# A new written-out order of loads and steps for a packed attention followed by a two-layer MLP

## The chip, the cores and the metric

The kernel runs on one core of a Trainium2 chip. Times are device microseconds (us) of one launch. The engines are TensorE (PE: matrix products; its weight loads are shown as PEld), VectorE (DVE), ScalarE (ACT), GpSimd (POOL) and SyncE (SP). POOL and SP only issue transfers here: POOL the loads, SP the transposing transfers within the chip's memory and the stores. Each engine works through its own queue in order.

## The reference

Eight batches, eight heads, 576 positions, head dimension 64, and 32 "pack" queries p per head:

```python
def sm_attn(qq, kk, vv):
    s = scale * np.matmul(qq, kk.transpose(0, 1, 3, 2))
    a = softmax(s)
    return np.matmul(a, vv)
p_packed = sm_attn(p, k, v)               # 32 rows per head
out = sm_attn(q, p_packed, p_packed)      # 576 rows per head
x = out.transpose(0, 2, 1, 3).reshape(B * S, H * D)   # 4608 x 512
r = np.maximum(x @ w_in, 0.0)             # 4608 x 2048
y = (s * (r * r) + b) @ w_out             # 4608 x 512, f32
```

## The kernel before

The work is a list of words, and each word is a step of one batch. The same function `run` reads the list and issues what the word says; each engine gets its part in the order of the list (the class `Pinned` and the helpers `mm` and `tr`, lines 62, 65 and 73, keep the program order). So the order of every queue is written out by hand, and a word that waits on an engine holds up all later words of that engine, but none of another.

The words, with the batch as first number:

- `Lk`, `Lq`, `Lv`, `Lp`, `Lpall`, `Lwi`, `Lwo`, `Lsb`: loads, issued by POOL. There is one raw buffer each for k, q and v, so a load waits until the batch before has been turned or copied out. Batch 0's loads come in two parts. `Lwi0.1` loads columns 0 to 256 of w_in, `Lwi2.4` 512 to 1024, and so on.
- `Tk`, `Tq`: k or q turned on PE (batches 0 and 1) into PSUM and copied out; `Dk`, `Dq`: turned by a transposing transfer on SP (batches 2 to 7).
- `PD`, `PP`, `PA`, `PPA`: the pack queries doubled and turned; `V`: v copied into the order that the products want (DVE).
- `F` first scores and their exponential (ACT); `P` packed values and their division (DVE); `X` packed values turned; `S` second scores and exponentials; `A` the softmax sums on PE, their logarithm and inverse on ACT, the product with the exponential on DVE. Batch 0 has `e`, `d`, `l`, `i`, `G` for the pieces of S and A.
- `W`: packed values times a quarter of w_in (an eighth in batch 0), copied out by two copies.
- `M` (and `h` in batch 0): 128 of the 2048 hidden columns: four products of 288 columns (h: of 384 where its last number is 0, of 192 where it is 1), a ReLU out of PSUM, a square on DVE.
- `O`: products with w_out for a tile of 128 rows, `xN` of its 16 steps; `Q`: the tile scaled, the bias added (DVE), and stored (SP, two stores a tile). The last tile is done in two halves of 256 columns.
- `BT`: the sums of w_out for the bias. `Z`: idle products on zeros.

`@` names the PSUM banks that a step takes (there are eight), and a trailing `a` or `v` says whether ACT or DVE does the copy or the ReLU. A word named again goes on with the same step: the first `M3.4@2` is its products, `M3.4a` its ReLU, the next `M3.4` its square. At most three ReLU results wait for their square (pool `ysp`), and at most five output tiles for their stores (pool `outp`).

PE's order in the long middle mixes `M` of batch b with `O` of batch b-1, and puts F, P, X, S, W and A of the next batch in between.

Of the kernel before, what the change touches and what calls it, by code (L numbers as in the profile page):

```python
# [14 lines left out]
def kernel(  # L15
# [670 lines left out]
    for word in """  # L686
        Tk0.0@2 Lq0.1 Tk0.0v Tk0.0v PD0 Z2@1 PP0@4 PP0v Tk0.1@6 PP0v Tk0.1a Tk0.1v Z2@5 F0.0@0 F0.0
        F0.1@2 F0.1 V0.0 Z3@4 P0.0@5 P0.0 V0.1 Z4@4 X0.0 X0.0v Z1@4 P0.1 P0.1 Z4@4 X0.1 Tq0.0@6 Tq0.0v
        Tq0.0v Tq0.1@4 S0.0.0@0 Tq0.1v Z2@2 S0.1.0@6 Lwi0.1 X0.1v Tq0.1a S0.1.1 e1.1 W0.0@4 e1.0 Z1@3
        d1.1@2 l1.1 Lp1 d1.0 S0.0.1 l1.0 Lwi6.8 PD1 PP1@6 PP1v e0.0 Z2@7 d0.0@2 PP1v e0.1 d0.1 Z4@7  # L690
        W0.6@0 W0.0v W0.0v W0.6v i1.1 W0.7@4 i1.0 l0.1 i0.1 G0.1 Lwi1.2 l0.0 Z5@6 W0.1@2 i0.0 G0.0 W0.6a
        W0.1a W0.1a G1.1 h0.12.0@0 W0.7a W0.7a h0.0.0@6 h0.0.0a Lwi2.4 G1.0 h0.14.1@2 h0.12.0v h0.12.0
        W0.2@4 W0.2a Lk1 W0.2a h0.14.1v Lv1 h0.2.0@0 h0.14.1 h0.14.0@6 h0.14.0a Lq1 h0.0.0 h0.2.0v
        h0.2.0 h0.4.1@2 h0.4.1v h0.14.0 W0.3@4 W0.3v W0.3a Lwi4.6 h0.4.0@0 h0.4.0a Tk1.0@6 Tk1.0v Tk1.0v
        Tk1.1@2 Tk1.1v Tk1.1a h0.0.1@4 F1.0@0 h0.0.1a F1.0 F1.1@6 h0.4.0 h0.4.1 h0.0.1 h0.6.0@2 h0.2.1@4
        V1 F1.1 h0.12.1@0 P1.1@6 P1.1 X1 h0.6.0a h0.2.1a h0.2.1 h0.12.1v h0.12.1 Lwo0.4 h0.6.1@2 Lsb
        Tq1.1@4 X1a h0.6.1v Tq1.1a Tq1.1a Tq1.0@6 Tq1.0v W1.0@0 h0.6.1 Tq1.0v W1.0v W1.0v S1@2,4 S1 S1
# [97 lines left out]
```

## Time and profile before

| | us |
|---|---|
| median of 3 runs | 250.53 (250.45 to 250.72) |
| the profiled execution | 250.68 |
| its span, first to last instruction | 248.9 |
| PE busy | 237.4 (95%) |
| DVE busy | 165.8 (67%) |
| ACT busy | 121.4 (49%) |
| first product of PE | 1.19 |
| last matrix product ends | 245.24 |

A line of the timeline gives the start, the time from the start of the first to the end of the last of its instructions, the engine, the line of the kernel, what it writes and reads, the shapes and the count; in brackets the idle time before and who ended it. In the list of waits, each line has the engine that waited, whom it waited for, the total, the number of waits and the longest. In the chain that ended last, each piece is the start, its length and the engine or transfer. A line's number can be that of a helper (L62 is every product, L73 every instruction of the other engines). The transfers' landing times that the text gives are those of the same trace.

### The profile page before, as it was taken

The numbers are of one execution on the slowest core, as the hardware profiler recorded it, in microseconds if no ns is written. First come the engines' busy times: TensorE is split into PE (matmuls) and PEld (weight loads), VectorE is DVE, ScalarE is ACT, GpSimd is POOL, SyncE is SP. The second block draws the span as 40 slices with busy tenths as digits, with TensorE's granted clock in tenths as the row PEclk, the third lists the DMA queues.
The fourth block names the chain that finished last, engine by engine and source line by source line (L and its number), as shares of the span: only waits on it lengthen the run. The fifth ranks groups of instructions, "written<-read, shape, count | busy, mean of one in ns | idle before, by whom it ended". The sixth has DMA issues, their size and how long they took to land.

```text
span 248.9 us, 5651 instructions
## 1 busy us (share of the span) xinstructions
PE 237.4 (95%) x2334; PEld 133.9 (54%) x2334; DVE 165.8 (67%) x336; ACT 121.4 (49%) x213; POOL 30.6 (12%) x45
## 2 busy tenths in 40 slices
PE   8889869999799999999999999999999999999994
PEld 3545644655355655476546645574547554675442
DVE  4657989799765856897469854983478724971232
ACT  2347768522464442675158423991278515890000
POOL 8643222001010210102003001020000000000000
PEclk9999999999999999999999999999999999999998
DMA  6999999997995999899999968969239031200135
GB/s 98 170 197 204 204 192 205 203 150 180 144 218 102 200 162 225 156 130 158 170 234 151 228 151 148 186 90 175 78 95 190 2 94 33 61 27 24 45 81 148
DMA packets 60522, 35.53 MB, mean 143 GB/s; under 512 B 32720, under 2 KB 56016, under 8 KB 60496
## 3 DMA queue, kind: packets, MB, share of 16 engines
q0 software_dynamic: 26272, 18.58, 52.8%
q1 hardware_dynamic: 34176, 16.55, 31.5%
q8 instruction: 18, 0.29, 0.5%
q14 instruction: 8, 0.07, 0.1%
q10 hardware_dynamic: 48, 0.03, 0.1%
HBM read 37.23 MB, written 9.44 MB: 187 GB/s over the span
## 4 chain that ended last, share of the span: by engine, by line
PE 76%; DVE 9%; DMA 8%; ACT 2%; POOL 2%; issue 2%; SPq 0%; POOLq 0%; ACTq 0%; DVEq 0%
PE banks L62 76%; DMA w_in_sb<-in_moe_w_in_dram 4%; DMA qT<-qn 3%; DVE gT L73 2%; DVE rlu L73 2%; ACT rlu L73 1%; DVE bias L73 1%; DVE pbd L73 1%; DVE biasrep L73 1%; ACT e L73 1%; POOL qn L73 1%; POOL kn L73 1%; POOL vn L73 1%; DVE ysb L73 1%; DVE kT L73 0%
## 5 line engine op out<-in xcount | busy, mean ns | idle before, releaser
L62 PE MATMUL banks<-w_out_sb,gT 128*128 128x512 bf16 (+1 forms) x592 | 140.9, 374 | 0.0
L62 PEld LDWEIGHTS <-gT 128*128 128x128 bf16 x592 | 55.7, 98 | 54.0 <-issue 4.5
L62 PE MATMUL banks<-aT,pw 128*128 128x288 bf16 (+2 forms) x512 | 74.1, 286 | 1.8 <-DVE rlu L73 0.7
L73 ACT ACTIVATE rlu<-banks 128x576 bf16<-128x576 f32 (+2 forms) x94 | 57.6, 656 | 33.1 <-PE banks L62 19.2
L73 DVE TENSOR_TENSOR gT<-rlu 128x576 bf16<-128x576 bf16 (+2 forms) x128 | 55.4, 454 | 12.7 <-ACT rlu L73 9.5
L62 PEld LDWEIGHTS <-pw 128*128 128x128 bf16 x512 | 49.2, 98 | 24.8 <-issue 2.2
L73 DVE SCALAR_TENSOR_TENSOR ysb<-banks,svec,biasrep 128x512 f32<-128x512 f32 (+1 forms) x37 | 26.8, 732 | 33.5 <-PE banks L62 33.1
L73 ACT ACTIVATE e<-banks 96x768 bf16<-96x768 f32 (+3 forms) x34 | 21.8, 693 | 49.1 <-PE banks L62 49.1
L73 DVE TENSOR_SCALAR rlu<-banks 128x576 bf16<-128x576 f32 (+2 forms) x34 | 25.1, 741 | 6.6 <-PE banks L62 2.9
L73 DVE CAST pw<-banks 128x512 bf16<-128x512 f32 (+1 forms) x37 | 22.3, 634 | 5.5 <-PE banks L62 5.4
L73 ACT CAST pw<-banks 128x512 bf16<-128x512 f32 (+1 forms) x35 | 16.4, 538 | 2.3 <-PE banks L62 2.3
L62 PE MATMUL banks<-zb 128*128 128x512 bf16 x42 | 12.9, 434 | 1.2 <-DVE zb L73 1.2
L73 POOL DMA_DIRECT2D qn<-in_q_dram x9 | 7.0, 776 | 52.5 <-DMA qT<-qn 49.5
L73 DVE TENSOR_TENSOR aT<-e,rcd 128x576 bf16<-128x576 bf16 (+2 forms) x18 | 11.8, 685 | 1.0 <-ACT rcd L73 1.0
L62 PE MATMUL banks<-w_in_sb,ppd 64*32 64x512 bf16 (+1 forms) x288 | 11.2, 357 | 0.9 <-ACT e L73 0.5
L62 PEld LDWEIGHTS <-ppd 64*32 64x32 bf16 x432 | 5.3, 89 | 11.7 <-issue 8.5
L73 POOL DMA_DIRECT2D vn<-in_v_dram x9 | 6.7, 748 | 39.2 <-DVE vr L73 37.4
L73 ACT ACTIVATE ld<-banks 128x576 f32<-128x576 f32 (+2 forms) x18 | 10.2, 596 | 1.6 <-PE banks L62 1.0
L73 POOL DMA_DIRECT2D kn<-in_k_dram x9 | 6.9, 768 | 31.9 <-DMA kT<-kn 28.3
L73 ACT ACTIVATE rcd<-ld 128x576 f32<-128x576 f32 (+2 forms) x18 | 10.7, 630 | 0.3
L73 DVE RECIPROCAL rd<-banks 128x2 f32<-128x2 f32 (+1 forms) x9 | 1.5, 170 | 11.1 <-PE banks L62 10.3
L73 DVE COPY vr<-vn 96x3072 bf16<-96x3072 bf16 (+1 forms) x9 | 7.7, 859 | 1.0 <-DMA vn<-in_v_dram 1.0
(54 smaller groups left out, 98.9 us busy)
## 6 DMA issues: line engine op xcount, KB each, us to landing
out_dram<-ysb SPq DMA_DIRECT2D x23, 192.0 KB, 2.8
kn<-in_k_dram POOLq DMA_DIRECT2D x7, 576.0 KB, 9.7
vn<-in_v_dram POOLq DMA_DIRECT2D x7, 576.0 KB, 11.4
qn<-in_q_dram POOLq DMA_DIRECT2D x7, 576.0 KB, 8.7
out_dram<-ysb SPq DMA_DIRECT2D x24, 128.0 KB, 3.4
w_out_sb<-in_moe_w_out_dram POOLq DMA_DIRECT2D x4, 512.0 KB, 15.4
w_in_sb<-in_moe_w_in_dram POOLq DMA_DIRECT2D x3, 512.0 KB, 12.4
out_dram<-ysb SPq DMA_DIRECT2D x23, 64.0 KB, 2.1
```

Source lines behind the costliest of these rows:

```text
L62: return tc.keep_in_program_order(nc.tensor.matmul(*a, **kw))
L73: return lambda *a, **kw: tc.keep_in_program_order(f(*a, **kw))
```

## The change

Nothing but the list changes, and with it line numbers by one. All steps that compute are there as before; what differs is the order, the banks, which of ACT and DVE does a copy or ReLU (M: 80 on ACT and 32 on DVE, 86 and 26 before; h: 13 and 3, 8 and 8 before), and the idle products (44 in all, the first 12 among them; 42 before). The order of the loads differs too. The opening, cut after the words in which batch 1 is under way:

```diff
-    Tk0.0@2 Lq0.1 Tk0.0v Tk0.0v PD0 Z2@1 PP0@4 PP0v Tk0.1@6 PP0v Tk0.1a Tk0.1v Z2@5 F0.0@0 F0.0
-    F0.1@2 F0.1 V0.0 Z3@4 P0.0@5 P0.0 V0.1 Z4@4 X0.0 X0.0v Z1@4 P0.1 P0.1 Z4@4 X0.1 Tq0.0@6 Tq0.0v
-    Tq0.0v Tq0.1@4 S0.0.0@0 Tq0.1v Z2@2 S0.1.0@6 Lwi0.1 X0.1v Tq0.1a S0.1.1 e1.1 W0.0@4 e1.0 Z1@3
-    d1.1@2 l1.1 Lp1 d1.0 S0.0.1 l1.0 Lwi6.8 PD1 PP1@6 PP1v e0.0 Z2@7 d0.0@2 PP1v e0.1 d0.1 Z4@7
-    W0.6@0 W0.0v W0.0v W0.6v i1.1 W0.7@4 i1.0 l0.1 i0.1 G0.1 Lwi1.2 l0.0 Z5@6 W0.1@2 i0.0 G0.0 W0.6a
-    W0.1a W0.1a G1.1 h0.12.0@0 W0.7a W0.7a h0.0.0@6 h0.0.0a Lwi2.4 G1.0 h0.14.1@2 h0.12.0v h0.12.0
-    W0.2@4 W0.2a Lk1 W0.2a h0.14.1v Lv1 h0.2.0@0 h0.14.1 h0.14.0@6 h0.14.0a Lq1 h0.0.0 h0.2.0v
-    h0.2.0 h0.4.1@2 h0.4.1v h0.14.0 W0.3@4 W0.3v W0.3a Lwi4.6 h0.4.0@0 h0.4.0a Tk1.0@6 Tk1.0v Tk1.0v
-    Tk1.1@2 Tk1.1v Tk1.1a h0.0.1@4 F1.0@0 h0.0.1a F1.0 F1.1@6 h0.4.0 h0.4.1 h0.0.1 h0.6.0@2 h0.2.1@4
-    V1 F1.1 h0.12.1@0 P1.1@6 P1.1 X1 h0.6.0a h0.2.1a h0.2.1 h0.12.1v h0.12.1 Lwo0.4 h0.6.1@2 Lsb
-    Tq1.1@4 X1a h0.6.1v Tq1.1a Tq1.1a Tq1.0@6 Tq1.0v W1.0@0 h0.6.1 Tq1.0v W1.0v W1.0v S1@2,4 S1 S1
-    W0.4@6 W0.4v Lpall Lwo4.8 W0.5@2 W0.5a W0.5v W0.4v Lwo8.12 W1.1@0 A1.0@4 W1.1a h0.10.0@2 W1.1v
-    A1.0 h0.10.1@6 h0.10.1a A1.1@0 A1.1 A1.1 h0.10.0v h0.8.1@4 h0.10.1 A1.0 Lwo12.16 W1.3@6 W1.2@2
-    O0.3x1@0 h0.8.1v O0.3x1 O0.1x1@1 W1.3a W1.3v O0.2x3@4 h0.8.1 O0.3x2 A1.1 O0.1x1 h0.8.0@6 O0.1x2
-    W1.2a W1.2a h0.8.0a h0.10.0 h0.6.0 A1.0 M1.0@2 M1.0a PA O0.2x1 h0.8.0 O0.1x1 M1.3@6 M1.6@2 M1.6v
-    O0.3x2 M1.6 M1.3a Lq2 M1.3 O0.2x1 M1.14@6 M1.14a M1.5@2 O0.3x1 M1.5v M1.5 O0.2x1 PPA0@5,6 M1.9@2
-    PPA0 O0.1x3 M1.9a M1.9 BT@7 M1.4@2 PPA0 O0.3x3 O0.2x1 M1.4a O0.0x2@5 O0.3x3 Lk2 O0.3x1 O0.0x5
 ...
+    Lq0.1 PD0 PP0@1 Tk0.0@2 Tk0.0a Tk0.0a PP0a Z2@0 Tk0.1@4 Tk0.1a PP0v Lp1 Tk0.1v V0.0 Z2@6 F0.0@2
+    F0.0 Z5@7 P0.0@0 P0.0 F0.1@4 F0.1 Lwi0.1 Z1@1 X0.0 X0.0v V0.1 Z4@1 P0.1 P0.1 Tq0.0@2 Tq0.0a
+    Tq0.0v Z2@1 Tq0.1@1 Tq0.1v Tq0.1a X0.1 X0.1v S0.0.0@6 Lwi2.4 Z1@4 S0.0.1 e0.1 S0.1.0@2 S0.1.1
+    Z3@5 d0.1@0 e0.0 d0.0 e1.1 e1.0 W0.0@4 d1.1@6 l0.0 PD1 W0.0v d1.0 l1.0 i1.0 G1.0 Z6@2 W0.3@2
+    W0.3v W0.3v l0.1 W0.2@0 Lwi6.8 W0.2v Z6@2 W0.7@2 l1.1 W0.6@6 i1.1 G1.1 W0.2a PP1@0 Lwi1.2 i0.1
+    G0.1 W0.0a i0.0 G0.0 W0.7a PP1v PP1a W0.7a h0.6.0@4 W0.6v W0.6a W0.1@0 W0.1a W0.1a h0.6.0v
+    h0.12.1@2 h0.6.0 h0.12.1a h0.12.1 h0.4.1@6 h0.14.0@4 h0.4.1a h0.14.0a h0.0.1@0 h0.0.1v h0.0.1
+    h0.14.1@2 h0.14.0 h0.4.1 h0.6.1@6 h0.4.0@4 h0.6.1a h0.6.1 h0.14.1a Lk1 Tk1.0@0 h0.4.0a Tk1.0v
+    Tk1.0v h0.14.1 h0.2.1@6 h0.2.1a h0.12.0@2 Lwi4.6 Tk1.1@4 Tk1.1a h0.4.0 h0.2.0@0 W0.5@6 h0.12.0a
+    Tk1.1v W0.4@4 W0.4a W0.4v h0.2.0a h0.2.1 h0.12.0 W0.5v F1.0@2 F1.0 h0.0.0@4 h0.0.0v W0.5a
+    h0.8.0@0 h0.8.0a F1.1@2 h0.10.0@6 Lv1 V1 h0.8.0 F1.1 P1.1@4 h0.2.0 h0.10.0a h0.0.0 h0.8.1@0
+    h0.8.1a h0.10.1@2 h0.10.1a Lq1 Tq1.0@6 Tq1.0a Tq1.0a P1.1 X1 X1v Tq1.1@0 Tq1.1v W1.0@2 W1.1@4
+    Tq1.1v W1.0v W1.0a S1@6,0 S1 S1 W1.3@2 W1.3v W1.3v Lwo0.4 O0.2x2@6 O0.1x2@7 Lpall O0.2x2 h0.8.1
+    A1.0@0 O0.0x3@2 W1.1a W1.1a A1.0 PA O0.0x1 A1.0 A1.0 O0.3x3@3 A1.1@4 A1.1 O0.1x1 Lwo4.8 PPA0@0,1
+    Lsb O0.0x1 h0.10.1 O0.0x1 O0.2x1 O0.1x1 O0.3x1 Lwo8.12 A1.1 A1.1 O0.1x2 M1.4@4 O0.3x3 Lwo12.16
+    PPA0 PPA0 O0.0x2 M1.4a M1.4 h0.10.0 O0.3x1 M1.2@4 O0.1x3 M1.2a M1.2 Lv2 W1.2@0 W1.2a BT@4 Lk2
+    Lq2 O0.1x1 W1.2v M1.6@0 M1.6a O0.1x1 O0.0x1 O0.1x1 Dk2 O0.3x7 M1.3@0 O0.3x1 M1.3a BT M1.5@4
+    O0.2x2 M1.1@0 M1.3 M1.5a M1.5 O0.2x3 M1.6 M1.1a M1.1 M1.8@4 M1.8a O0.2x2 M1.15@0 O0.2x1 M1.15a
+    V2 O0.0x2 M1.15 M1.0@4 Dq2 PPA0 Q0.3 O0.0x2 M1.0a M1.0 M1.9@0 M1.9a M1.9 M1.14@4 M1.14a O0.0x3
+    Q0.0 O0.2x3 M1.7@0 Lq3 Q0.2 F2.0@4 M1.7v M1.8 F2.1@2 O0.1x1 F2.0 M1.7 O0.1x3 M1.10@0 M1.14 F2.1
+    P2.1@6 Lk3 M1.10a P2.1 M1.13@4 M1.13a M1.13 M1.12@2 M1.12a X2 M1.11@0 M1.11a X2v O1.4x2@4 Q0.1
+    O1.4x2 PPA0 O1.0x1@5 W2.2@2 W2.2v W2.2v S2@0,6 S2 S2 M1.11 O1.0x2 O1.4x1 O1.0x2 M1.10 A2.0@0
 ...
```

Further on, from the second scores of batch 2 (S2; in the new list it is in the last line above) to the first scores of batch 3 (F3.0):

```diff
-    M1.15@2 Dk2 Q0.3 O0.1x4 O0.0x1 M1.10v O0.0x2 M1.14 O0.2x2 O0.1x1 M1.10 V2 O0.2x1 Dq2 O0.0x1
-    O1.0x1@0 M1.15v M1.15 O0.2x2 F2.0@6 F2.0 F2.1@2 F2.1 O0.1x2 Q0.0 O0.1x1 Q0.2 M1.2@4 P2.1@6 M1.2a
-    Q0.1 M1.12@2 M1.12a M1.8@4 P2.1 M1.2 X2 O1.0x3 M1.8v M1.8 X2a W2.2@2 W2.2v W2.2v S2@6,4 S2 S2
-    O1.4x2@1 O1.0x2 M1.11@6 Lv3 A2.0@2 A2.0 A2.0 O1.4x3 M1.7@4 M1.7a M1.11v O1.3x1@6 M1.11 A2.1@2
-    A2.0 O1.4x1 O1.3x2 Lq3 PPA0 M1.13@4 M1.13v O1.3x1 O1.1x3@7 M1.12 A2.1 W2.1@2 W2.1a W2.1v M1.7
-    W2.0@4 O1.1x1 O1.0x1 O1.4x1 O1.1x2 A2.1 W2.0a W2.0a O1.1x1 M1.13 O1.1x2 A2.1 O1.1x2 Lk3 Dk3
-    M2.0@2 M2.0a O1.0x1 M2.10@4 M2.10a M2.10 O1.4x1 O1.1x2 W2.3@2 M2.2@4 M2.2v Dq3 O1.1x2 M2.2
 ...
-    O2.0x1 Q1.2 Dq4 F3.0@4 F3.0 F3.1@2 O2.0x3 O2.2x1@0 F3.1 O2.0x2 P3.1@6 P3.1 O2.0x5 X3 X3v O2.2x3
 ...
+    A2.0 A2.0 A2.1@2 O1.1x1@6 M1.12 O1.3x2@7 W2.0@0 W2.0v W2.0v O1.0x1 Lv3 O1.1x6 W2.3@0 A2.0 Dk3
+    A2.1 A2.1 A2.1 W2.1@2 W2.3a W2.3a O1.4x1 O1.3x2 Lk4 O1.3x1 O1.4x2 M2.10@0 O1.1x1 O1.3x2 M2.10v
+    O1.1x1 M2.10 O1.1x2 O1.0x2 O1.1x1 M2.0@0 W2.1v W2.1a O1.0x2 O1.1x1 M2.0v M2.0 V3 M2.5@2 M2.5a
+    M2.8@0 M2.8a M2.8 O1.3x2 M2.7@2 O1.0x3 M2.7a M2.7 O1.0x1 M2.2@0 M2.2a O1.4x1 M2.2 Lv4 F3.0@2
+    F3.0 O1.3x2 O1.1x1 M2.4@0 M2.1@2 O1.3x1 M2.1v M2.1 M2.4a O1.0x2 M2.6@0 Q1.0 M2.6a M2.6 O1.4x2
+    O1.1x1 M2.5 O1.1x1 O1.4x2 M2.15@2 M2.15a M2.15 M2.12@0 M2.12a M2.12 O1.3x2 O1.4x1 M2.11@2 M2.3@0
+    M2.11a PPA0 Dq3 M2.3a Q1.1 O1.2x1@5 Lq4 O1.2x1 M2.4 M2.13@2 M2.13v M2.13 PPA0 O1.2x1 O1.4x1 PPA0
+    O1.2x1 F3.1@0 M2.3 F3.1 O1.2x1 M2.9@2 M2.9a M2.9 O1.2x2 O2.0x1@6 P3.1@0 V4 O1.4x1 Q1.4 P3.1
 ...
```

The end:

```diff
 ...
-    O7.4x4 M7.12 O7.4x5 O7.3x4 O7.4x3 Q7.4 O7.4x4@6 O7.2x1 O7.4x1 O7.0x2@7 O7.2x2 O6.2x2 O7.3x1
-    O7.0x3 O7.3x7 O7.0x1 O7.2x1 O6.2x1 O6.3x1@4 O7.0x3 O6.2x2 O7.0x2 O7.3x2 Q7.3 O6.2x3 O6.3x1
-    O7.2x1 O7.0x2 Q6.2 O7.1x1@3 O7.2x3 O7.1x1 O7.2x1 O6.3x2 O7.1x2 O6.3x2 O7.2x5 Q7.2 O6.3x3 O7.1x1
-    O6.3x1 O7.1x1 O6.3x1 O7.1x1 O6.3x1 O7.0x3 O6.3x3 Q7.0 O6.3x1 O7.1x1 Q6.3 O7.1x8 O7.4x4 Q7.1
-    O7.4x7 Q7.4
+    M7.7v O6.1x2 M7.7 O7.0x2@3 O7.4x3 M7.6 O7.2x1 M7.11@6 M7.8 O6.1x1 Q6.1 O7.4x1 O7.1x1 O7.4x1
+    M7.11a O7.1x1 O7.2x2 O7.4x1 O7.1x1 M7.11 O7.1x1 M7.12@6 M7.12v O7.1x4 O7.2x5 O7.3x3@0 O7.0x1
+    O7.3x1 O7.4x1 O7.3x2 O6.2x1 O7.3x2 O7.0x3 O7.2x2 O7.4x1 O6.2x1 O7.4x2 O6.3x1@6 O7.0x1 O7.3x3
+    O6.2x2 O7.3x1 M7.12 O7.3x1 O7.1x1 O7.0x6 O6.3x2 O7.4x4 O7.2x1 O7.4x1 O7.0x2 Q7.4 O7.4x1@7 O7.0x1
+    O7.2x2 O6.3x2 O7.2x2 O6.3x2 O7.3x1 O6.3x1 O7.3x2 O7.4x1 O6.3x4 Q7.2 O6.3x1 Q6.2 Q7.3 O6.3x3
+    O7.4x2 O7.1x4 Q7.0 O7.4x3 Q6.3 Q7.1 O7.4x9 Q7.4
```

## The prediction, made before the changed kernel had run

> **What bounds the kernel now.** I read the page's first part, then the busy time by stage, the waits of TensorE (PE), the chain that ended last, and the timelines of PE and of SP's queue.
>
> ```profile
> PE 237.4 (95%) x2334; PEld 133.9 (54%) x2334; DVE 165.8 (67%) x336; ACT 121.4 (49%) x213; POOL 30.6 (12%) x45
> ```
>
> PE is the bound by far. By stage (columns: window, its length, then busy time and count of each engine, granted PE clock, DMA):
>
> ```profile
> 0.00:20.00 20.00, 17.23 (x224) 8.62 (x225) 10.28 (x36) 7.37 (x16) 12.91 (x22) 1.00 1.16 158
> 20.00:45.00 25.00, 21.59 (x309) 13.63 (x308) 22.23 (x49) 18.62 (x37) 6.14 (x8) 1.00 1.32 201
> 45.00:68.00 23.00, 21.39 (x229) 11.66 (x227) 20.79 (x39) 7.94 (x15) 0.83 (x2) 1.00 1.01 165
> 68.00:245.00 177.00, 177.00 (x1578) 100.00 (x1576) 112.04 (x212) 87.45 (x148) 10.70 (x14) 1.00 0.73 130
> 245.00:249.00 4.00, 0.23 (x3) 0.00 (x0) 0.48 (x1) 0.00 (x0) 0.00 (x0) 0.80 0.46 135
> ```
>
> From 68 us on PE never pauses. A better order of work can gain only before 68 us, where VectorE (DVE) is busy 22.23 of 25 and ScalarE (ACT) 18.62, and at the very end; anywhere between it can only lose. "Busy" hides pauses, so I price PE by start-to-start times:
>
> ```profile
> 50.50 3.83 PE L62 MATMUL banks<-w_out_sb,gT 128*128 128x512 bf16 x17
> 54.17 0.65 PE L62 MATMUL banks<-aT,pw 128*128 128x288 bf16 x4
> 54.66 1.03 PE L62 MATMUL banks<-w_out_sb,gT 128*128 128x512 bf16 x4
> ```
>
> A 512-wide product costs (54.17 - 50.50)/17 = 0.216 us, a word M (four 288-wide) 0.49. Pricing every word so (h with u=0 0.65, u=1 0.33, F 0.35, A 0.245, P 0.49) gives 217.8 us of useful PE work, idle products left out, in either order. PE ends at 245.24; so 245.24 - 217.77 = 27.5 us are **lost**: start, idle products, waits. I count lost time at fixed points. At S2 (second scores of batch 2, start 67.40) the useful work is 43.7 (68 O words' products 14.65, 13 M 6.37, h 7.8, all else 14.9), so 23.7 is lost, 23.8 once S2 has begun. The other 3.65 comes later, and is the price of switching to the small-tile products: about 0.09 before each P and S group, 0.09 + 0.12 around each W group. The waits behind the loss:
>
> ```profile
> PE banks L62 <- DMA qT<-qn: 1.1, 1, 1.1
> PE banks L65 <- DVE pk L73: 1.0, 1, 1.0
> PE banks L62 <- DVE rlu L73: 0.7, 1, 0.7
> PE banks L62 <- DVE ysb L73: 0.5, 1, 0.5
> ```
>
> ```profile
> 59.02 8.34 DMA qT<-qn
> ...
> 67.40 32.84 PE banks L62 x276
> ...
> 207.88 37.36 PE banks L62 x259
> 245.24 0.02 issue
> 245.26 0.48 DVE ysb L73
> ```
>
> The last wait of PE ends at 67.40, on a transposing DMA of batch 2's q that took 8.34 us; then PE runs to the end.
>
> **The change, part by part.**
>
> *Idle products*: 44 for 42, 2 x 0.216 = +0.4 us if they replaced nothing; they stand where PE would wait anyway, and are inside the lost time below. The first 12 are the same and end at 5.68.
>
> *Loads*: POOL's order changes, the bytes don't, and landings in this stage follow one another without a gap. By the trace's landing times vn lands at 9.6 and 11.1, qn at 13.1 and 14.25, unmoved. Lp1 goes ahead of the first w_in (+0.16: pn landed so much behind it). Of w_in, 256:1024 comes before 1536:2048, together in by 22.4 as now. Lwi4.6 moves ahead of Lv1 and Lq1: in by 28.6 (34.5 now), which makes vn1 31.5 (29.0) and qn1 34.5 (32.0). w_out's four parts still end at 47.1; pall is ahead of the second. In batch 2 v goes first and q last: v2 50.0, k2 53.0, q2 55.9.
>
> *Evictions* in the opening go from DVE to ACT: of the h ReLUs 13 on ACT and 3 on DVE (8 and 8), batch 0's k copies 3 and 1 (1 and 3). With durations from the rows (wide rlu 0.95 DVE, 0.81 ACT; narrow 0.55, 0.49; kT 0.45, 0.64) the sum up to the first product with w_out, at 18.8 us of useful work in both orders, goes from DVE 28.1 and ACT 24.4 to DVE 24.5 and ACT 27.8. The longer of the two hardly falls, so this alone is no gain; the order must bring it.
>
> *Walk through the opening* (each start is the latest of: the word before on PE, the bank read out, the operand there). F0.0 8.1 (8.3 now; two k copies and one p copy run in a row on ACT, 6.3 to 7.95). P0.0 10.26, on vn, as now. F0.1 now follows it, so P0.1 slips from 11.96 to 12.4; Tq0.0 starts at 13.1, on qn, as now. Then W0.0 17.5; an idle group in bank 2 waits till 19.7 for W0.3's copies; the first h waits for the inverse and weigh steps (ACT to 21.8, DVE to 22.4) and starts at **22.45, where it is 21.41 now: one us worse**. From there ACT sets the pace: exponentials of F1.1 end at 33.9 by full durations, some 32.7 if two ACT instructions in a row overlap by the 0.1 us that rows such as pw x4 in 1.20 (mean 378 ns) show. P1.1 follows. Tq1.0 must wait for qn1 (34.5), the first O for w_out (37.0): it starts at 37.2 to 38.5 with 18.75 done, lost 18.5 to 19.8 (39.42 with 18.81 now, 20.6). BT needs the last w_out (47.1) with 27.6 done: lost 19.5 to 20.0. Behind BT its 4.9 us of DVE work (50.69 to 55.54 now) hold the squares of M1.3, M1.5, M1.6; PE has other work and waits about 0.3. The transposes: k2 issues 53.1, lands 58.1 as now; q2 issues right behind, before any store, and with no load in flight (POOL's next needs its buffer): about 61.2. S2 is reached at 65.6, **lost 20.2 where it is 23.8: -3.6 us**. Of that 1.3 is the qT wait, 0.8 to 2.1 the stretch to the first O, the rest the ysb and bank waits. If I erred at 22.45 by an us it is mostly caught by the waits for w_out.
>
> *Steady stage*: 217.77 - 45.4 of work, as many switches (7 + 12 for W, 5 P, 5 S: 3.5 against 3.5). DVE's sum over any 6 us of PE work is at most 6.3, ACT's 6.3 (7.9 and 7.2 now), so their load is flatter. But F3.0 comes at 58.3 of useful work, 78.8 us, now 96.7; it needs k3 transposed. q3, k3, v3 are issued at 61.3 to 63; k3 lands about 72.5 (9.7 us for the second of two and 11.5 for the second of three now). What its transpose costs depends on what flies beside it:
>
> ```profile
> 78.89 2.39 SPq L73 DMA_TRANSPOSE kT<-kn  x1
> ...
> 95.41 6.12 SPq L73 DMA_TRANSPOSE kT<-kn  x1
> ```
>
> The first, with no load beside it, landed after 5.9, the second, with v4 and q4 in flight, after 9.7, 3.5 after q4. So k3's lands between 76.5 and 83.5; I take 79.3 (3.5 after v3 at 75.8): a wait of **+0.5**, from 0 to 4.7; on PE all that follows (O1.3, M2.4, M2.1) stands behind it, and ACT and DVE then run dry for as long. Later ones have more room: Dq3 lands at 91 to 93 for S3 at 94.5, Dk4 at 105 to 108 for F4.0 at 112. SP's stores stand behind these transposes; five ysb buffers cover a block of some 7 us.
>
> *End*: six output tiles leave in the last 5.5 us of PE (Q7.2, Q6.2, Q7.3, Q7.0, Q6.3, Q7.1), now three or four. SP's two stores of a tile take 0.8 us alone (244.84 to 245.63) and 1.07 in a row (242.04 to 244.23: 2.19 for four). From -4.7 before PE's end: 0.8 + 5 x 1.07 puts the last half tile's store 1.5 after PE's end, now 0.53: **+1.0**, between 0 (all at 0.75) and 1.1.
>
> *Clock*: the Trainium skill's "TensorE: Matmul & The Clock Gate" (Part 1, The HAM clock gate) says that an idle window of about 3.4 us halves the clock, and Part 4 that transposes don't count as busy, which speaks against an opening with more holes. The row: 96-wide transposes 42 ns apart (12 in about 0.5 us), full speed, around waits of up to 1.1 us. My holes are 0.5 to 1.1 us; so nothing is charged; one slow window would add about 1.7.
>
> *Sum*: span 248.88 - 3.6 + 0.5 + 1.0 = 246.8. The profiled run took 250.68, 1.8 beyond its span, so 248.6; the median is 0.15 lower: **248.5 us**.
>
> **Rivals.** (a) *The batch 3 transpose is late*: lands at 83.5, wait 4.7 in place of 0.5, 252.7; it decides from a landing at about 81.4, where the gain is gone. For: 6.12 above, 8.34 for q2 under loads. Against: only v3 flies beside. (b) *ACT becomes the opening's bound*: its 27.8 us serve later than I walk, only the qT wait and a little more go: lost 22.0 at S2, 250.2. For: 35 ACT instructions in a row from the first exponential to F1.1; against: the overlap. (c) *More gain*: no wait at F3.0, no store backlog: 246.9.
>
> **Numbers.** Forecast 0.55 (247.5 to 249.5), (a) 0.18 (from 250 up), (b) 0.15, (c) 0.12. Under 0.2%, 0.5 us, a time is not told from no change. Faster: 0.55 + 0.12 + half of (b); slower: 0.15 of (a); the rest same. Range 246.7 to 251.6.
>
> **What would show it.** PE's first h product at 22.4; first w_out product at 37 to 38.5; no qT wait at S2, near 65.6; F3.0 at 79 with a DMA kT wait under 1; PE full to about 241.7; the last store on SP 1.5 after it. I am wrong if a wait on kT or kn above 2 us stands between 70 and 115, if 512-wide products in the opening stand 427 ns apart, as the first ones do, or if an M waits for rlu at each step.

## The result, and the profile after

| | before | after |
|---|---|---|
| median of 5 runs each | 250.53 us | **248.24 us** (247.54 to 248.59) |
| ratio after to before | | 0.9908, 95% interval 0.9882 to 0.9933 |
| the profiled execution | 250.68 | 247.68 |
| its span | 248.88 | 245.90 |
| last matrix product ends | 245.22 | 240.41 |
| from there to the end of the span | 3.66 | 5.49 |

The kernel is 0.9% faster; 248.5 was forecast. PE ends 4.8 us earlier, and 1.8 us of that are given back behind PE's end. Here and below, medians are over all executions; ratios and intervals leave out those that took over 1.5% more than the fastest of the same kernel.

The first part of the page of the kernel after, and its busy time by stage, with the columns as before (window, length, busy time and count of PE, PEld, DVE, ACT and POOL, PE clock, DMA):

```profile
PE 237.0 (96%) x2336; PEld 134.1 (55%) x2336; DVE 163.8 (67%) x330; ACT 126.9 (52%) x219; POOL 30.6 (12%) x45
```

```profile
0.00:20.00 20.00, 18.02 (x225) 8.93 (x226) 9.59 (x33) 10.55 (x22) 13.34 (x22) 1.00 1.15 162
20.00:45.00 25.00, 23.59 (x325) 14.92 (x324) 20.17 (x46) 21.14 (x42) 5.71 (x8) 1.00 1.33 201
45.00:68.00 23.00, 23.00 (x247) 13.04 (x246) 19.28 (x39) 13.83 (x22) 2.31 (x3) 1.00 1.10 192
68.00:245.00 177.00, 172.41 (x1544) 97.22 (x1541) 114.73 (x215) 81.38 (x135) 9.20 (x12) 1.00 0.67 129
```

PE's busy time over the whole run is the same (237.0 for 237.4). From 20 to 45 us PE is busy 23.59 of 25 us for 21.59, and from 45 to 68 all of 23 for 21.39: the gain is there. In the first of these two stages ACT rose from 18.62 to 21.14 and DVE fell from 22.23 to 20.17, so that the two carry about the same. In the last row PE ends at 240.41, so 172.41 is every us it had.

The waits of PE in the kernel after (left out are the one ahead of the first idle products, 1.2 us in both kernels, and a last one of 0.2):

```profile
PE banks L62 <- DVE pw L73: 0.6, 2, 0.4
PE banks L62 <- DVE vr L73: 0.5, 2, 0.3
PE banks L62 <- DMA w_in_sb<-in_moe_w_in_dram: 0.2, 1, 0.2
PE banks L62 <- ACT rlu L73: 0.2, 1, 0.2
```

The four waits of before (on q2's transpose 1.1, on pk 1.0, on the ReLU 0.7, on ysb 0.5) are gone. Behind the first idle products no single wait of 0.5 us is left.

SP's queue in the kernel after, from the timeline: the start, the time from first to last, and the transfer.

```profile
52.62 2.99 SPq L73 DMA_TRANSPOSE kT<-kn  x1
55.73 3.03 SPq L73 DMA_TRANSPOSE qT<-qn  x1
58.80 6.56 SPq L73 DMA_DIRECT2D out_dram<-ysb  x8
71.70 3.19 SPq L73 DMA_TRANSPOSE kT<-kn  x1
```

The second line is batch 2's q. It now goes out directly behind k, ahead of eight stores, and by its landing time it was there at 60.36, four us before S2 needs it (64.41; 67.40 before). The last line is batch 3's k: it landed at 76.76, and F3.0 started at 77.95 without a wait.

The end, DVE's and SP's part of the timeline:

```profile
233.38 9.53 SPq L73 DMA_DIRECT2D out_dram<-ysb  x15
```

```profile
234.92 2.73 DVE L73 SCALAR_TENSOR_TENSOR ysb<-banks,svec,biasrep 128x512 f32<-128x512 f32 x4 [1.57 <-DMA out_dram<-ysb]
238.72 0.75 DVE L73 SCALAR_TENSOR_TENSOR ysb<-banks,svec,biasrep 128x512 f32<-128x512 f32 x1 [1.07 <-DMA out_dram<-ysb]
240.10 1.14 DVE L73 SCALAR_TENSOR_TENSOR ysb<-banks,svec,biasrep 128x512 f32<-128x512 f32 x2 [0.63 <-DMA out_dram<-ysb]
```

Four whole tiles come in a row; the fifth and the sixth (the first of the last row, whose second is the half tile) wait for the landing of an earlier store, because all five output buffers are taken. From 235.70 SP issues 12 stores up to the start of the thirteenth at 242.53 with no pause: 0.57 us each, 1.14 a tile. The last store on SP is issued 2.1 us after PE's end; before, 0.5. The chain that ended last shows the same: PE is on it until 232.87, and then stores and the output tiles, where before it was PE up to 245.24:

```profile
199.60 33.24 PE banks L62 x232
232.87 0.49 DVE ysb L73
...
237.50 2.47 DMA out_dram<-ysb
240.10 0.75 DVE ysb L73
```

Where the 3 us of the two spans are, by lost time (the time less the useful PE work up to that point, counted as in the prediction):

| point | before | after | difference |
|---|---|---|---|
| first h | 15.18 | 15.21 | 0.0 |
| P1.1 | 17.32 | 17.10 | -0.2 |
| S1 | 18.70 | 17.67 | -1.0 |
| first product with w_out | 20.62 | 18.59 | -2.0 |
| BT | 21.37 | 18.77 | -2.6 |
| P2.1 | 22.16 | 18.88 | -3.3 |
| S2 | 23.70 | 19.00 | -4.7 |
| PE's end | 27.47 | 22.65 | -4.8 |
| end of the span | | | -3.0 |

### The profile page after: what moved, and what is told of

Its sections match the earlier page's. It is cut to its first block, busy times and chain, and to the rows that moved or that the text cites. A ratio compares the mean times of both kernels' runs of the same rounds, so it can differ in the third digit from the quotient of the medians.

```text
span 245.9 us, 5657 instructions
## 1 busy us (share of the span) xinstructions
PE 237.0 (96%) x2336; PEld 134.1 (55%) x2336; DVE 163.8 (67%) x330; ACT 126.9 (52%) x219; POOL 30.6 (12%) x45
## 4 chain that ended last, share of the span: by engine, by line
PE 83%; DMA 7%; DVE 3%; POOL 3%; ACT 1%; issue 1%; DVEq 0%; SPq 0%; POOLq 0%
PE banks L62 81%; DMA w_in_sb<-in_moe_w_in_dram 5%; DMA out_dram<-ysb 2%; PE banks L65 1%; DVE ysb L73 1%; POOL qn L73 1%; POOL w_in_sb L73 1%; DVE gT L73 1%; POOL kn L73 1%; POOL vn L73 1%; DVE pw L73 0%; DVE vr L73 0%; DVE rlu L73 0%; ACT rlu L73 0%; POOL pn L73 0%
## 5 line engine op out<-in xcount | busy, mean ns | idle before, releaser
L62 PE MATMUL banks<-w_out_sb,gT 128*128 128x512 bf16 (+1 forms) x592 | 144.2, 374 | 0.0
L73 ACT ACTIVATE rlu<-banks 128x576 bf16<-128x576 f32 (+2 forms) x93 | 58.2, 648 | 56.9 <-PE banks L62 41.4
L62 PEld LDWEIGHTS <-gT 128*128 128x128 bf16 x592 | 55.9, 98 | 49.5 <-issue 5.2
L62 PE MATMUL banks<-aT,pw 128*128 128x288 bf16 (+2 forms) x512 | 77.1, 286 | 0.2 <-ACT pw L73 0.2
L73 DVE TENSOR_TENSOR gT<-rlu 128x576 bf16<-128x576 bf16 (+2 forms) x128 | 54.6, 453 | 18.4 <-ACT rlu L73 17.1
L73 DVE TENSOR_SCALAR rlu<-banks 128x576 bf16<-128x576 f32 (+2 forms) x35 | 26.4, 759 | 12.2 <-PE banks L62 9.8
L73 DVE CAST pw<-banks 128x512 bf16<-128x512 f32 (+1 forms) x34 | 20.5, 630 | 6.8 <-PE banks L62 6.7
L73 ACT CAST pw<-banks 128x512 bf16<-128x512 f32 (+1 forms) x38 | 18.7, 541 | 4.5 <-PE banks L62 4.4
L73 ACT ACTIVATE rcd<-ld 128x576 f32<-128x576 f32 (+2 forms) x18 | 11.3, 631 | 0.4
L62 PEld LDWEIGHTS <-kT 128*128 128x128 bf16 x192 | 7.7, 98 | 3.3 <-issue 0.7
L62 PE MATMUL banks<-pbd,kT 128*128 128x64 bf16 x192 | 8.3, 193 | 0.2 <-ACT rlu L73 0.2
```

The costliest lines, as they stand in the source:

```text
L62: return tc.keep_in_program_order(nc.tensor.matmul(*a, **kw))
L73: return lambda *a, **kw: tc.keep_in_program_order(f(*a, **kw))
```

## The experiments

The theory: the gain comes from the order in the opening (transposes, loads, word order), not from the shift of evictions to ACT; the end gives back what SP's row of stores takes; the early F3.0 costs nothing as long as k3's transpose comes in time. The rivals, one for each part, are named in the expectations.

### The second transpose alone, in the kernel before

```diff
-    M1.15@2 Dk2 Q0.3 O0.1x4 O0.0x1 M1.10v O0.0x2 M1.14 O0.2x2 O0.1x1 M1.10 V2 O0.2x1 Dq2 O0.0x1
+    M1.15@2 Dk2 Dq2 Q0.3 O0.1x4 O0.0x1 M1.10v O0.0x2 M1.14 O0.2x2 O0.1x1 M1.10 V2 O0.2x1 O0.0x1
```

> The order of before, with one word moved: Dq2 (q of batch 2, transposed on SP) stands right behind Dk2, ahead of the stores of Q0.3. Theory (PE's wait at S2 is that transfer standing behind stores and flying beside v3's load; lost PE time is never made up): q2 lands near 61, not 67.4, PE has no qT wait at S2, and the kernel takes 1.2 less than before: 249.3. Rival (another wait steps into its place, on the exponentials or on kT): S2 starts within 0.4 us of 67.4 and the time is 250.2 to 250.6.

249.84 us (10 runs; before on the same chip 250.58; 249.3 was expected), ratio 0.997 (0.995 to 0.9989). SP's part of its timeline:

```profile
53.98 2.97 SPq L73 DMA_TRANSPOSE kT<-kn  x1
57.08 3.02 SPq L73 DMA_TRANSPOSE qT<-qn  x1
60.14 6.30 SPq L73 DMA_DIRECT2D out_dram<-ysb  x8
```

The wait for qT is gone from the list of PE's waits; S2 starts at 66.16 with 22.46 lost (23.70 before), and PE ends at 244.00 for 245.22, with the same 3.7 us behind it. So in the profiles the 1.2 us saved at S2 is carried whole to the end (the medians differ by 0.7), and one word of the list is worth about a quarter of the -4.7 at S2. How the other 3.5 us divide among loads, word order, banks and copies was not tried apart.

### The shift of evictions alone, in the kernel before

Five of the narrow h ReLUs go to ACT, so that 13 are on ACT and 3 on DVE as in the kernel after; the order stays. (The copies of k that also change engine stay as they were.)

```diff
-    W0.2@4 W0.2a Lk1 W0.2a h0.14.1v Lv1 h0.2.0@0 h0.14.1 h0.14.0@6 h0.14.0a Lq1 h0.0.0 h0.2.0v
-    h0.2.0 h0.4.1@2 h0.4.1v h0.14.0 W0.3@4 W0.3v W0.3a Lwi4.6 h0.4.0@0 h0.4.0a Tk1.0@6 Tk1.0v Tk1.0v
+    W0.2@4 W0.2a Lk1 W0.2a h0.14.1a Lv1 h0.2.0@0 h0.14.1 h0.14.0@6 h0.14.0a Lq1 h0.0.0 h0.2.0v
+    h0.2.0 h0.4.1@2 h0.4.1a h0.14.0 W0.3@4 W0.3v W0.3a Lwi4.6 h0.4.0@0 h0.4.0a Tk1.0@6 Tk1.0v Tk1.0v
...
-    V1 F1.1 h0.12.1@0 P1.1@6 P1.1 X1 h0.6.0a h0.2.1a h0.2.1 h0.12.1v h0.12.1 Lwo0.4 h0.6.1@2 Lsb
-    Tq1.1@4 X1a h0.6.1v Tq1.1a Tq1.1a Tq1.0@6 Tq1.0v W1.0@0 h0.6.1 Tq1.0v W1.0v W1.0v S1@2,4 S1 S1
+    V1 F1.1 h0.12.1@0 P1.1@6 P1.1 X1 h0.6.0a h0.2.1a h0.2.1 h0.12.1a h0.12.1 Lwo0.4 h0.6.1@2 Lsb
+    Tq1.1@4 X1a h0.6.1a Tq1.1a Tq1.1a Tq1.0@6 Tq1.0v W1.0@0 h0.6.1 Tq1.0v W1.0v W1.0v S1@2,4 S1 S1
...
-    O0.3x1@0 h0.8.1v O0.3x1 O0.1x1@1 W1.3a W1.3v O0.2x3@4 h0.8.1 O0.3x2 A1.1 O0.1x1 h0.8.0@6 O0.1x2
+    O0.3x1@0 h0.8.1a O0.3x1 O0.1x1@1 W1.3a W1.3v O0.2x3@4 h0.8.1 O0.3x2 A1.1 O0.1x1 h0.8.0@6 O0.1x2
```

> The order of before with five narrow ReLUs of batch 0 (h0.14.1, h0.4.1, h0.12.1, h0.6.1, h0.8.1) moved from DVE to ACT, so 13 on ACT and 3 on DVE as in the changed order; nothing else. Theory (the shift alone is no gain, the order brings it): first O at 39.0 to 39.9 (39.4 before), time 250.1 to 251.1. Rival (DVE was the opening's bound, and the shift is the gain): first O 1 us earlier or more, time 249.4 or less.

250.77 us (10 runs; before 250.3), ratio 1.0009 (0.9981 to 1.0036): no change that can be measured. Busy time from 20 to 45 and 45 to 68 us:

```profile
20.00:45.00 25.00, 20.88 (x305) 13.29 (x305) 19.85 (x44) 20.00 (x41) 6.13 (x8) 1.00 1.32 201
45.00:68.00 23.00, 22.06 (x232) 12.48 (x235) 20.75 (x39) 9.21 (x16) 1.72 (x3) 1.00 0.99 161
```

DVE and ACT are level at 19.85 and 20.00, as in the kernel after, and PE is not busier for it (20.88; 21.59 before; some 30 of the 592 records of products with w_out are missing from this trace, so the starts tell more). The first product with w_out starts at 39.07 for 39.42 and BT at 49.32 for 49.02. Here an engine that is busy 22 of 25 us was relieved and the path did not move. (Its profile reaches S2 at 66.43, because q2's transpose happened to land 1.2 us earlier in that execution.)

### The opening's idle products left out

All idle products behind the first twelve are removed from the kernel after (32 products); the output is not touched by them.

```diff
-        Lq0.1 PD0 PP0@1 Tk0.0@2 Tk0.0a Tk0.0a PP0a Z2@0 Tk0.1@4 Tk0.1a PP0v Lp1 Tk0.1v V0.0 Z2@6 F0.0@2
-        F0.0 Z5@7 P0.0@0 P0.0 F0.1@4 F0.1 Lwi0.1 Z1@1 X0.0 X0.0v V0.1 Z4@1 P0.1 P0.1 Tq0.0@2 Tq0.0a
+        Lq0.1 PD0 PP0@1 Tk0.0@2 Tk0.0a Tk0.0a PP0a Tk0.1@4 Tk0.1a PP0v Lp1 Tk0.1v V0.0 F0.0@2
+        F0.0 P0.0@0 P0.0 F0.1@4 F0.1 Lwi0.1 X0.0 X0.0v V0.1 P0.1 P0.1 Tq0.0@2 Tq0.0a
...
```

> The changed order without its 32 idle products in the opening (the first 12 stay). Theory (they fill time in which PE waits anyway, and PE keeps its speed over holes of some 2 us): all later words start within 0.3 us of their times, 248.0 to 248.5. Rival (holes let the clock fall): products of 384 columns in the opening stand 320 ns apart in place of 162 for 3 us or more, and the time is 1 to 3 us longer.

252.42 us (248.98 to 255.66 over ten executions), ratio 1.0039 (1.0001 to 1.0077), where the kernel after has 0.9908 and, in a second set, 0.9932: some 3 us more by the ratios, 4 by the medians. So the idle products don't only stand in waits: without them the clock falls. The mean granted clock was 0.954 to 0.971 in all ten executions, and 0.996 to 0.999 in the five of the kernel after. The profiled execution took 254.47. Two stretches of its busy time, the granted clock in the last column but two:

```profile
11.40:25.05 13.65, 10.08 (x148) 5.78 (x148) 7.53 (x20) 8.96 (x24) 6.51 (x8) 0.50 1.37 200
25.05:127.40 102.35, 99.46 (x1058) 57.77 (x1079) 73.23 (x147) 62.08 (x105) 11.29 (x15) 1.00 1.09 175
```

PE ran at half clock for 13.65 us, four windows of 3.41 us, and again for one window at 130.87. Not all that was lost stems from the slow opening itself. Against the first profile of the kernel after, PE is 1.35 us late at the first product with w_out (38.69 for 37.34) and 1.7 at S2. The rest comes further on: it is 2.8 late at F3.0 (80.71 for 77.95) and 5.3 at 130.30 (125.03), with a wait at each, and 6.9 at PE's end, behind the second slow stretch.

```profile
80.71 0.52 PE L62 MATMUL banks<-pbd,kT 128*128 128x64 bf16 x12 [0.89 <-DMA kT<-kn]
...
130.30 3.90 PE L62 MATMUL banks<-w_out_sb,gT 128*128 128x512 bf16 x10 [2.12 <-DVE ysb L73]
```

The last experiment on k3 meets the same two places. So the theory, that these products only fill time in which PE waits anyway, is refuted. What the two more of the changed order cost or bring was not tried apart.

### The end: where the 1.8 us is

First, the second store of each of the last six tiles goes to ACT's queue, which is idle there.

```diff
-                store(self.ysb, d0, d1, i0, b, col, n, act if d0 else sp)
+                store(self.ysb, d0, d1, i0, b, col, n, act if d0 or self.late else sp)
...
+    for x in ((7, 2), (6, 2), (7, 3), (7, 0), (6, 3), (7, 1)):
+        todo[x].late = True
```

> The changed order, with the second store of each of the last six whole tiles (Q7.2, Q6.2, Q7.3, Q7.0, Q6.3, Q7.1) issued by ACT, which is idle by then, and not by SP. Theory (the end is set by SP issuing 13 stores in a row): the last store on SP comes 0.6 after PE's end in place of 2.1, time 246.7. Rival (the five ysb buffers set the end: Q6.3 and Q7.1 wait for the landing of stores): DVE still waits about 1 us for stores, and the time falls by 0.5 or less.

247.91 us (246.66 to 248.08), ratio 0.9898 (0.9866 to 0.9931), where the kernel after has 0.9908: the interval can't tell them apart. The theory's 246.7 did not come; the rival's wait is there. In the profile the last store on SP is issued 1.26 us after PE's end, not 0.6, and the time behind PE's end falls from 5.49 to 4.73. DVE's last tiles:

```profile
239.60 0.75 DVE L73 SCALAR_TENSOR_TENSOR ysb<-banks,svec,biasrep 128x512 f32<-128x512 f32 x1 [0.94 <-DMA out_dram<-ysb]
241.49 1.14 DVE L73 SCALAR_TENSOR_TENSOR ysb<-banks,svec,biasrep 128x512 f32<-128x512 f32 x2 [1.14 <-PE banks L62]
```

The fifth tile still waits for a store to land. The sixth starts at 241.49, later than PE needs it: a store of ACT issued at 237.38 landed at 241.30 and held the buffer 3.9 us, where the stores of the same stretch on one queue took 1.9 to 2.8. (The row names PE; PE had been done, and the store came last.) The Trainium skill's "DMA: Bandwidth & Descriptors" (Issuing engines are not separate DMA queues) says that a second issuing engine saves only the time to issue. Here that is what it brought: the issues came sooner, the landings later.

Second, seven output buffers in place of five, one queue:

```diff
-    outp = ctx.enter_context(tc.tile_pool(name="outp", bufs=5))
+    outp = ctx.enter_context(tc.tile_pool(name="outp", bufs=7))
```

> The changed order with seven ysb buffers in place of five, all stores on SP as they were. Theory (SP's row of stores alone sets the end): DVE's waits on stores at Q6.3 and Q7.1 go, but the last store still comes 1.9 to 2.1 after PE's end: at most 0.2 us gained. Rival (the buffers set it): the last store comes 1.2 after PE's end or earlier, 0.9 us gained.

248.27 us (247.57 to 250.1), ratio 0.9929 (0.9893 to 0.9965), beside 0.9932 for the kernel after in the same set. In its timeline DVE waits for no store any more:

```profile
235.65 9.54 SPq L73 DMA_DIRECT2D out_dram<-ysb  x15
...
240.32 0.75 DVE L73 SCALAR_TENSOR_TENSOR ysb<-banks,svec,biasrep 128x512 f32<-128x512 f32 x1 [0.40 <-PE banks L62]
```

and yet SP takes the same 9.54 us for its 15 stores (9.53), and the last one is issued 2.15 us after PE's end (2.12). So it is as the theory had it: with one queue, SP's row binds, and more buffers alone gain nothing.

Third, both of these edits together:

> Both at once: the second store of each of the last six whole tiles on ACT, and seven ysb buffers. With two queues alone Q7.1 waited for the landing of Q6.2's store on ACT (3.9 us after its issue). Theory now (two limits, queue and buffers, of which each alone holds the end near 5 us): the span ends 3.6 to 3.8 us after PE's last product, as before the change, not 5.5: 246.4. Rival (stores land slower with two queues, so nothing is left): 4.6 or more, 247.3 or above.

246.57 us (246.23 to 249.35), ratio 0.9849 (0.982 to 0.9877). On another chip again:

> The same kernel as in the earlier run with both ends (second stores on ACT, seven output buffers). Theory: 246.6 again, ratio to before 0.983 to 0.987, the time behind PE's end 4.0 to 4.6, in place of 5.5. Rival: the first figure was a lucky set of executions: 247.9, as with the second stores on ACT alone.

246.70 us (246.47 to 248.18; before there 249.86), ratio 0.988 (0.9819 to 0.9941). In the first set the kernel after stood beside it with 248.34 us:

> The changed order itself, once more, beside the three below. It tells how much its own time moves from execution to execution, and whether a window at half clock in the opening, as one execution of the variant with k3 behind v3 had at 9.1 to 12.5 us, belongs to that variant alone. If to the variant: granted clock 0.996 to 1.000 in all executions and 248.0 to 248.5. If to the changed order: some executions at 0.993 or below, and longer by 1.5 to 2.5 us each.

(0.9932, 0.9908 to 0.9956; the intervals don't meet.) So this version beats both kernels, by 1.8 us and 3.7 us in that set. The timeline of its second profile:

```profile
233.63 7.89 SPq L73 DMA_DIRECT2D out_dram<-ysb  x9
...
235.95 5.83 ACTq L73 DMA_DIRECT2D out_dram<-ysb  x7
...
240.69 0.48 DVE L73 SCALAR_TENSOR_TENSOR ysb<-banks,svec,biasrep 128x256 f32<-128x256 f32 x1 [0.56 <-PE banks L62]
```

PE ends at 240.66, the last half tile follows at once, and the last SP store goes out 0.55 us after PE's end, as in the kernel before. The time behind PE's end is 4.27 (4.59 in the first profile), not the 3.6 to 3.8 that I first expected: the last pair landed 2.5 and 2.7 us after its issue, and nine of the twelve stores before it 2.7 to 4.0 us after theirs.

The repeated run of the kernel after also shows how much the opening varies with the loads: in that execution (249.28) PE waited 1.2 for qn1 and 0.5 for w_out, both later than in the first profile (qn1 at 35.10 for 33.67, w_out's last part at 48.58 for 46.68), and 24.2 was lost at PE's end for 22.65. The gain by PE's end is then 3.2 and not 4.8 us. That is one reason why the medians differ by 2.3 and the first two profiles by 3.0.

The question about the clock stays open. Three of the ten executions had a mean granted clock below 0.996 (0.994, 0.993 and 0.992), but this sign can't tell. The profiled one, at 0.994, has full clock until 244.55, 2.6 us behind PE's last product, so its clock fell after the work; and the shortest of the ten, 247.47, is the one with 0.993. Whether the longest, 250.25 at 0.992, had a slow window inside is not known.

### Is F3.0 close to waiting?

In the kernel after k3's transpose landed 1.2 us before F3.0. To see what lateness costs, k3 is loaded behind v3.

```diff
-        P2.1@6 Lk3 M1.10a P2.1 M1.13@4 M1.13a M1.13 M1.12@2 M1.12a X2 M1.11@0 M1.11a X2v O1.4x2@4 Q0.1
+        P2.1@6 M1.10a P2.1 M1.13@4 M1.13a M1.13 M1.12@2 M1.12a X2 M1.11@0 M1.11a X2v O1.4x2@4 Q0.1
...
-        A2.0 A2.0 A2.1@2 O1.1x1@6 M1.12 O1.3x2@7 W2.0@0 W2.0v W2.0v O1.0x1 Lv3 O1.1x6 W2.3@0 A2.0 Dk3
+        A2.0 A2.0 A2.1@2 O1.1x1@6 M1.12 O1.3x2@7 W2.0@0 W2.0v W2.0v O1.0x1 Lv3 Lk3 O1.1x6 W2.3@0 A2.0 Dk3
```

> The changed order, with one load moved: k of batch 3 is loaded behind v of batch 3, not ahead of it. It tests the price of rival (a). Theory (no slack behind F3.0): k3 lands near 74.5 in place of 71.6, its transpose near 79.5 to 80, F3.0 waits from 77.9 for 1.6 to 2.0 us, and all of it shows at the end: 248.2 + 1.7 = 249.9. Rival (later waits swallow it, as at the loads of w_out in the opening): a wait of that size at F3.0, but at most 0.5 us more in all.

251.96 us (249.65 to 255.19), ratio 1.0032 (0.9997 to 1.0067). Its profile could not say why. PE waited 1.8 us for batch 0's second k load in that execution, and a window at half clock followed (9.11 to 12.53), so that everything was shifted by 2.3 us and F3.0 found its operand just landed:

```profile
PE banks L65 <- DMA kn<-in_k_dram: 1.8, 1, 1.8
```

So it was run once more:

> The same kernel as in the earlier run with k3 loaded behind v3, since that profile was disturbed in the opening. If the wait is real: F3.0 waits for the transposed k3 by 1 to 2 us (Dk3 issued about 75 and landed about 80, F3.0 ready at about 78), all later work shifts by it, time 249.4 to 250.3. If the gap behind the transpose is hidden: no wait on kT between 70 and 90, time 248.2. A rival for the first run's excess: the half-clock window in its opening comes from the moved load; it cannot, since that load comes 50 us later; so no such window is expected here more often than in the kernel itself.

252.53 us (252.23 to 254.37; before 249.86), ratio 1.0112 (1.0056 to 1.0169): slower than the kernel before, some 4 us above the medians of the kernel after, where I expected 1 to 2. The profiled execution, 254.37, is the longest of the four. Its opening has no window at half clock (15.21 lost at the first h), although the load is moved here too. PE, SP and DVE in its timeline:

```profile
80.19 0.52 PE L62 MATMUL banks<-pbd,kT 128*128 128x64 bf16 x12 [2.07 <-DMA kT<-kn]
...
130.05 3.40 PE L62 MATMUL banks<-w_out_sb,gT 128*128 128x512 bf16 x9 [2.23 <-DVE ysb L73]
...
120.69 6.92 SPq L73 DMA_TRANSPOSE kT<-kn  x1
...
127.71 0.96 DVE L73 COPY vr<-vn 96x3072 bf16<-96x3072 bf16 x1 [4.28 <-DMA vn<-in_v_dram]
```

and its clock around the second wait:

```profile
127.28:130.69 3.41, 1.18 (x12) 0.40 (x5) 2.98 (x5) 2.46 (x5) 0.47 (x1) 1.00 0.88 208
130.69:134.10 3.41, 3.41 (x10) 1.35 (x9) 1.35 (x3) 0.00 (x0) 0.30 (x1) 0.50 0.73 93
```

Three costs follow one another. F3.0 waits 2.1 us for kT, as expected. Fifty us later DVE stands 4.28 us at the copy of batch 5's v, which landed at 127.68 where it landed at 119.63 in the kernel after; the output tile queued behind that copy is late, and so is the PSUM bank that the next O words need: PE waits 2.2. That empties the clock's window of 3.41 us to 1.18 us of products, and the next window runs at half clock (products 0.43 apart in place of 0.216): the lost time grows by another 1.68, from 25.74 to 27.42. In all 29.34 is lost at PE's end, 6.7 more than in the kernel after. The other three executions, 252.23 to 252.70, are some 2 us shorter, and one of them (252.37) had a granted clock of 0.999, so it had no slow window: most of the cost does not need the clock.

The load is late by more than the shift because each load waits for its raw buffer, and that for a transpose. Batch 3's q transpose, issued 2.3 us later, ran beside the whole load of batch 4's v, held SP's queue 6.10 us for 3.82 and landed at 95.26 for 89.21. Batch 4's q could be loaded only then, and batch 4's k transpose came at 105.45 for 99.69. So batch 5's loads were issued from 111.64 on for 106.15, and then flew beside the k transpose, which took 6.92 for 3.53. The same wait at the same words (2.12 us at 130.30) and the same half-clock window appear in the profile without idle products. That the late transposes cause it there too was read from the issue times only, and not tried alone. In the first profile with both ends (249.35, the longest of its five), where no load is moved but the opening was about 1 us late, DVE stood 2.59 us at the same copy and PE 0.5. So loads and transposes can meet without the moved load too; but not every late start brings it: the profile with seven buffers, 2.3 us late from BT on, has no wait there.

## Why the prediction was right, and where it was not

**Idle products, loads.** The landing times held: vn1 30.80 (31.5 predicted), qn1 33.67 (34.5), w_out 46.68 (47.1), v2, k2 and q2 49.56, 52.52 and 55.42 (50.0, 53.0, 55.9). All were 0.4 to 0.8 us early. (One reading was wrong, without effect: in the new list only columns 512 to 1024 of w_in come before 1536 to 2048; 256 to 512 come last.)

**"This alone is no gain; the order must bring it."** The first half is shown by the run with the five ReLUs on ACT. Of the second, the place of q2's transpose is shown (1.2 us); the rest follows only because nothing else was changed.

**Walk through the opening.** Right in kind, too small in size: -4.7 at S2 for -3.6. The first h started at 21.55, not at 22.45. The walk added full durations for ACT up to 21.8, but the inverse of batch 0 had ended at 20.54: neighbours on ACT overlap there as they do later. "If I erred at 22.45 by an us it is mostly caught by the waits for w_out" is what happened: the first product with w_out came at 37.34 and BT at 46.40, at the near end of 37.2 to 38.5 and before the 47.1 of the last part, which BT doesn't need for its first products. In three other profiles of this opening w_out landed 1.3 to 2.6 us later and BT did wait, 0.5 to 1.8 us. So my term was that of a later landing, and the medians lie nearer to it than the first profile. The qT wait of 1.3 was the surest term and measured 1.2 by itself.

**F3.0, +0.5.** It was 0. The term took "3.5 after v3" for k3's transpose, from the case with loads beside it; it landed 5.06 after its issue, near the free case of 5.9, and only 2.2 after v3. The mechanism of rival (a) is real, as the moved load shows, and its price was put too low in one respect: "later ones have more room" holds for the kernel as it is, but not once F3.0 is late. I counted a lateness of PE as a plain shift; in the run it came back at 127 us and once more through the clock. My price for a slow window, 1.7 us, was measured as 1.68.

**The end, +1.0.** The mis-sized term: +1.8. The sum had a slip: 2.19 us for the four stores of two tiles is 1.10 a tile and not 1.07, and it stops at the end of the last store, before the next is issued. From 4.7 us before PE's end, as I placed it, 12 stores took 6.83 us, where my sum had 0.8 + 5 x 1.07 = 6.15. The price of a tile in a row is 1.14 and not 1.07, and the first tile is no cheaper, for the row has no start: it is 0.7 us of the difference, the later landing the rest. Five output buffers, which I held for enough, were used up too, but the run with seven shows that they cost nothing as long as SP's row stands.

**Clock.** No charge was right for the kernel as it is: full clock from 5.65 to 244.59. But my ground, that the holes are short, holds only with the idle products in them. The Trainium skill's "TensorE: Matmul & The Clock Gate" (Part 1, The HAM clock gate) speaks of a window of about 3.4 us without work; in the runs here a window with some work in it was enough, as the last section tells. That transposes don't count as busy, as I took from Part 4, does not fit the windows here either: the window from 4.57 to 7.98 of the run without idle products held 1.96 us of work, 1.09 of it transposes, and full clock followed, while 1.18 and 1.29 us without any transpose were followed by half clock.

**Sum.** 246.8 for the span was forecast, 245.9 came: -1.1 in the opening, -0.5 at F3.0, -0.1 in the steady stage, +0.8 at the end. The median was 248.24 for 248.5. That they lie so close is in part luck: the errors have opposite signs, and the median is 0.6 above the profiled execution. ("PE full to about 241.7" left out the +0.5 of the same sum.) Rival (b), ACT as the bound, is refuted: PE's waits on ACT are under 0.5 us in all. Rival (c) was half right: no wait at F3.0, but a backlog of stores.

## What to carry to other kernels

Look for the wait that ends last in the stage where the bound engine pauses, and see whether one transfer stands behind others in a queue: moving q2's transpose ahead of two stores kept its 1.2 us to the end in the profiles (0.7 in the medians), while a level load on two busy engines brought nothing. Count the work that leaves in the last microseconds, store by store: a finer mix up to the end means that many outputs become ready together, and both the issuing queue and the buffers must be widened at once, since either alone bought nothing that could be told. A written-out order whose loads wait for buffers has little slack to spare: a late operand of 2 us cost about 4 us in the medians of two sets and 6.7 in the profiled execution, where it made later loads meet transposes, so give the first of a chain of transfers its margin.

## What the runs showed of the hardware that I had not expected

- The granted clock changes at steps of 3.41 us (it stood for 3.41, 13.65, 105.8 and 238.9 us at a time: 1, 4, 31 and 70 steps). Windows with 1.18, 1.29 and 1.57 us of PE work (transposes included) were followed by a window at half clock; windows with 1.97, 2.07 and 2.35 were not. Between these, PE's busy time does not sort them. The first row below, of the run without idle products, was followed by half clock; the second, of the run with seven buffers, was not, and neither was a window with 1.51 us at the end of the first run with k3 moved (241.22 to 244.63). So no threshold comes out of these runs.

```profile
7.98:11.40 3.42, 1.89 (x59) 1.41 (x55) 1.54 (x4) 1.78 (x3) 1.69 (x3) 1.00 1.34 187
...
45.57:48.98 3.41, 1.85 (x23) 0.58 (x23) 1.70 (x4) 1.24 (x2) 0.00 (x0) 1.00 1.31 203
```

- It took more than that to come back: windows with 1.27, 2.50 and 2.90 us busy at half clock were followed by half clock again, those with 3.20 and 3.41 by full clock.
- Leaving out the idle products of the opening cost some 3 us (4 in the medians), although they are only 7 us of PE work and stand where PE waits. In the one profile, 1.4 us of it came in the opening at half clock, and the rest where the late PE met late loads.
- A transpose of k held SP's queue 2.6 to 3.5 us in the kernel after, and 6.92 us beside the last two of batch 5's loads in the run with k3 moved.
- In the last stretch the stores landed 1.9 to 2.8 us after their issue from one queue, and up to 4.4 us from two.
